# One-hot transfers on a second queue, rounding planned by SyncE's clock, and another key tile in a borrowed buffer

## The chip, the core and the metric

The kernel runs on one core of a Trainium2 chip. The core has TensorE (PE: matrix products and transposes, into PSUM), VectorE (DVE), ScalarE (ACT), GpSimd (POOL) and SyncE (SP), each with its own instruction order, and 16 DMA engines. An instruction waits for semaphores, and all that stands behind it on the same engine waits too. The time is that of one execution on the device in microseconds; the median of a few executions is compared.

## The reference

Attention with routing by clusters, followed by a bilinear feed-forward block. Queries, keys and values are 4 batches x 8 heads x 768 positions x 64.

```
q_assign = argmax(q_n . c_n);  k_assign = argmax(k_n . c_n)     # 16 clusters per head
scores = where(q_assign == k_assign, q k^T / 8, -1e9)
attn = softmax(scores);  x = attn v                             # (B,H,S,D) -> (3072, 512)
out = ((x @ w_a) * (x @ w_b)) @ w_out                           # 512 -> 1536 -> 512
```

A query sees only the keys of its own cluster. The weights w_a, w_b and w_out come as 64-bit numbers and are rounded to 32 bits in the kernel.

## The kernel before

**Pairs of heads.** Two heads are worked on together, which gives 16 pairs. The first six (ND, line 167) are "dense": all 768 x 768 scores are made, the mask is added by a product of one-hot rows, and the exponential is taken. The other ten are "sorted": the rows are scattered by cluster into DRAM (L1509, POOL), loaded again in order (L1539, L1543), small score blocks are made (L1581), weighed (L1606, L1615), written back (L1635) and gathered (L1646).

**A dense pair** has two halves of 384 queries and, for each, six key tiles of 128 (j = 0 to 5). Two key tiles make a group: the scores L592, first by the one-hot rows ohT and then by qkT, into two PSUM tiles; the exponential L605 on ScalarE into a tile pt; the weighing with v, L634; the running sum of the exponentials on VectorE, L623. The tile of the exponential comes from `prob_room` (L579): four buffers of the pool ptp and, for every fifth tile, a stretch of xT that is not in use yet. At the end of a half the denominators are summed (L654) and inverted and applied on VectorE (L674 to L687).

**Pairs 4 and 5** (`by_blocks`) are prepared in 32 x 32 blocks on VectorE: L514 turns queries and keys, L405 makes the similarities, L518 turns these, L522 makes the one-hot rows and L530 turns them. Their 16 rows for each head and quarter then have to go to other partitions, to where the scores read them: eight small DMA transfers for a pair, `move_one_hot` (L492 to L497), all issued by SyncE. The index a is the head of the pair.

**Rounding.** 36 parts of the weights, 128 x 512 each, in the order of `weight_parts` (L1983): eight alternating parts of w_a and w_b for each third of the columns, then w_out's parts 5 to 11 and 0 to 4. For each a DMA into one of two buffers named raw (L300), then on VectorE L311, L314, L318, L321 and L329, and on ScalarE L325 and L326. I call the i-th rounding Ri, counting from 0. A buffer is loaded again when L321 and L325 have read it.

**Feed-forward.** For batch 0 an up product L727 with w_a is copied by ScalarE (L780) and multiplied on VectorE by the product with w_b (L784, which writes h): 24 pairs of products, in two blocks of 384 rows. Then come 21 down products from h and w_out. The first (p1, L1039) adds up over w_out's parts 0 to 5. It carries out all roundings that are left before it is written (`with_weights`, L1770). Later batches use sums of weight blocks kept in DRAM.

**The planner.** The order on each engine is written out by the Python program, with a clock of its own. `now` is the planned time of TensorE. Every engine has a planned clock in `clocks` (V, S, G, P for VectorE, ScalarE, GpSimd and SyncE), which each instruction issued through a `Clocked` object moves on by a fixed cost. Steps of the sorted pairs and roundings are events: `next_round` (L1823) lets rounding i into the order once `arrived[i]` plus a margin has passed and VectorE's clock allows it (`may_round`, L1814), and otherwise asks again 0.5 later. `loaded` (L1795) issues the load of a part and sets `arrived`. So a different planned cost or margin changes which instruction stands behind which, on all engines. SyncE's order holds all plain loads and stores, the reloads of the sorted pairs among them.

Of the kernel before, what the change touches and what calls it, by code (L numbers as in the profile page):

```python
# [34 lines left out]
P = 128  # L35
# [4 lines left out]
def kernel(  # L40
# [91 lines left out]
    with ExitStack() as fast:  # L132
        short_path(nc, tc, fast, c, cn, centroids_in, casts, n_far, q, k, v,
                   moe_w_a, moe_w_b, moe_w_out, out)
# [23 lines left out]
def short_path(nc, tc, ctx, c, cn, centroids_in, casts, n_far, q, k, v,  # L158
# [3 lines left out]
    B, H, S, D = q.shape  # L162
    NC = 16
    DM, DF = moe_w_a.shape
    NJ = S // P
# [5 lines left out]
    HB = S // 2  # L171
# [4 lines left out]
    now, last = [0.0], [0.0]  # L176
    clocks = {"V": 0.0, "S": 0.0, "G": 0.0, "P": 0.0}
    state = (clocks, now, last)
    V, Vs, Vc, Vh, Vm, Vl, Vd = (Clocked(nc.vector, "V", us, *state)
                                 for us in (0.56, 0.19, 0.29, 0.44, 0.7, 0.83, 0.96))  # L180
    S_, Ss, Sl = (Clocked(nc.scalar, "S", us, *state) for us in (0.5, 0.3, 0.85))
    Gi = Clocked(nc.gpsimd, "G", 1.28, *state)
    Q_, Qr, Qc = (Clocked(nc.sync, "P", us, *state) for us in (0.42, 0.62, 2.0))

    def pool(name, bufs, space=None, stack=ctx):
# [108 lines left out]
    raws = {}  # L294

    def load_w(i):
        if i >= len(w_parts):
            return
        raw = rawp.tile([P, WN], INT64, name="raw")
        Q_.dma_start(out=raw, in_=w_parts[i][1])  # L300
        raws[i] = raw
# [79 lines left out]
    qkTs, ohTs, sims = {}, {}, {}  # L381
# [110 lines left out]
    def move_one_hot():  # L492
        while to_move:
            p, ohT, kq, a = to_move.popleft()
            r = 32 * kq + a * NC
            Qr.dma_start(out=ohTs[p][a * D:a * D + NC, kq * HB:(kq + 1) * HB],
                         in_=ohT[r:r + NC, :])  # L497

    def prep_by_blocks(p):

# [28 lines left out]
        def one_hot_across():  # L529
            V.transpose(out=ohT, in_=oh.rearrange("p g c -> p (g c)"))  # L530
            to_move.extend((p, ohT, kq, a) for kq in (0, 2, 3, 1) for a in range(2))
            at(clocks["V"] + 0.6, lambda t: move_one_hot())
# [44 lines left out]
        return p, hf, j  # L577

    def prob_room(u):  # L579
        if u % 5 < 4:  # L580
            return ptp.tile([P, 2, HB], FP32, name="pt")
        return xTs[1][:, HP - 2].rearrange("p (a t) -> p a t", a=2)

    def score(us):
# [17 lines left out]
        def exp():  # L602
            for u, s in zip(us, tiles):
                pt = prob_room(u)
                Sl.activation(out=pt, in_=s[:, :, 0:HB], func=AF.Exp,  # L605
                                     scale=SCALE)
                probs[u] = pt
# [506 lines left out]
    def at(t, f):  # L1114
        heapq.heappush(events, (t, next(serial), f))
# [5 lines left out]
    def begin():  # L1121
        last[0] = now[0]
# [106 lines left out]
    def was(what, n, after=0.0):  # L1229
        return n < 1 or (what, n) in done and done[what, n] + after <= now[0]  # L1230
# [564 lines left out]
    def loaded(i):  # L1795
        while i > done_to[0]:
            done_to[0] += 1
            load_w(done_to[0])
            arrived[done_to[0]] = clocks["V"] if done_to[0] > 21 else now[0]

    done_to = [1]
    arrived = {}

    def round_one(i):
        loaded(i)
        round_w(i)
        if i < 20:
            at(last[0] + 2.5, lambda t: loaded(i + 2))
        else:
            loaded(i + 2)  # L1810
# [3 lines left out]
    def may_round(i):  # L1814
        idle = clocks["V"] <= now[0] + 0.6
        if i < 16:
            return idle or now[0] > 140 + 8.0 * (i - 8) and clocks["V"] <= now[0] + 2.0
        if i < 24:
            return idle or bool(is_late)
        return clocks["V"] <= now[0] + 1.4 and (  # L1820
            was("after", EARLY, 4) if i < 31 else was("put", EARLY - 1, 2))

    def next_round(t):  # L1823
        if not rounds:
            return
        i = rounds[0]
        if not (i in raws and arrived[i] + (4.5 if i < 22 else 3.5) <= now[0] and may_round(i)):
            at(now[0] + 0.5, next_round)
            return
        rounds.pop(0)  # L1830
        begin()
        round_one(i)
        at(max(t + 3.5, now[0]), next_round)

    at(98.0, next_round)
    for n in range(1, NSORT):
        sorted_pair(n, STARTS[n])
# [43 lines left out]
    for g in range(NG + 7):  # L1881
        p, l = divmod(g, GPP)
        if l == 0:
            move_one_hot()
            ready = prep_steps(p + 1)
# [344 lines left out]
```

## Time and profile before

| | us |
|---|---|
| median of 3 runs | 952.77 (952.34 to 955.7) |
| profiled execution | 951.85 |
| its span | 950.1 |
| TensorE busy | 928.4 (98%) |
| VectorE busy | 612.5 (64%) |
| ScalarE busy | 261.5 (28%) |
| POOL busy | 372.8 (39%) |

A row of a timeline reads: start, duration, engine, line and operation, what is written from what, partitions x elements and type, count, and in brackets the idle time of the engine just before with the instruction that ended it. Times count from the start of the span. Rows of a queue (SPq, ACTq) are DMA issues, and their duration is the issuing, not the transfer. A matmul row can hold several matmuls. TensorE's granted clock is 1.00 when it isn't throttled.

### The profile page before, as it was taken

The page shows a single profiled execution, that of the slowest core. Times are in us where ns is not written, and L with a number is a line of the kernel's source. Part 1 is how long each engine was busy: PE and PEld are TensorE (multiplying, and loading weights), DVE is VectorE, ACT ScalarE, POOL GpSimd, SP SyncE. Part 2 cuts the span into 40 slices and gives each one's busy share as a digit, 9 for nine tenths or more (in the row PEclk, how much of TensorE's full clock was granted, in tenths as well). Part 3 has the DMA queues.
Part 4 walks back from the last instruction along what each step waited for, and adds up shares of the span by engine and source line. Part 5 has one row for each costly group of instructions (what it writes and reads, how often), then busy time and mean ns, then how long its engine had stood idle before and what let it go on. Part 6 is the DMA issues. An engine that isn't in the chain of part 4 may idle for free.

```text
span 950.1 us, 20918 instructions
## 1 busy us (share of the span) xinstructions
PE 928.4 (98%) x8068; PEld 492.4 (52%) x8068; DVE 612.5 (64%) x1309; ACT 261.5 (28%) x564; POOL 372.8 (39%) x373
## 2 busy tenths in 40 slices
PE   8999989999999999999999999999999999999997
PEld 5454433434544567554545676545455664444564
DVE  5899988986869886759575945574354433333542
ACT  5876544633433301122212010212221001211100
POOL 1026645665554564555564545555553200000000
PEclk9999999999999999999999999999999999999999
DMA  8967675556799945784688548383825112122311
GB/s 196 243 177 198 175 219 137 161 172 160 185 218 177 206 145 127 158 179 111 147 150 180 165 98 193 96 184 100 165 55 160 37 57 63 56 61 61 113 35 32
DMA packets 293755, 131.82 MB, mean 139 GB/s; under 512 B 230032, under 2 KB 274832, under 8 KB 293648
## 3 DMA queue, kind: packets, MB, share of 16 engines
q1 hardware_dynamic: 281712, 114.23, 49.2%
q0 software_dynamic: 11520, 15.75, 6.1%
q8 instruction: 66, 1.08, 0.5%
q10 hardware_dynamic: 416, 0.43, 0.1%
q14 instruction: 41, 0.34, 0.1%
HBM read 86.93 MB, written 43.20 MB: 137 GB/s over the span
## 4 chain that ended last, share of the span: by engine, by line
PE 80%; DVE 12%; DMA 3%; SPq 2%; issue 2%; ACT 1%; POOL 0%; DVEq 0%; POOLq 0%; ACTq 0%
PE m L727 64%; PE s L592 3%; PE s L1581 3%; PE s L1606 2%; PE O L634 2%; DVE acc L623 2%; PE s L1615 2%; DVE rest L321 1%; PE s L1661 1%; PE m L405 1%; PE O L1367 1%; DVE rest L318 1%; DMA raw<-in_moe_w_out_dram 1%; PE m L654 1%; PE m L1356 1%
## 5 line engine op out<-in xcount | busy, mean ns | idle before, releaser
L1646 POOL DMA_INDIRECT xT<-od,idx x120 | 123.2, 1027 | 110.1 <-PE m L727 80.8
L727 PE MATMUL m<-xT,wa_sb 128*64 128x384 f32 x672 | 116.6, 488 | 2.2 <-DVE h L784 1.4
L727 PE MATMUL m<-xT,wb_sb 128*64 128x384 f32 x672 | 116.5, 488 | 1.3 <-DVE h L784 1.3
L902 DVE TENSOR_TENSOR ha<-ha,m 128x384 f32<-128x384 f32 x72 | 39.7, 551 | 88.0 <-PE m L727 68.4
L899 ACT COPY h<-m 128x384 f32<-128x384 f32 x72 | 34.4, 478 | 194.6 <-PE m L727 194.6
L727 PE MATMUL m<-wo_sb,h 128*64 128x256 f32 x768 | 87.1, 380 | 0.3 <-DVE wo_sb L329 0.3
L902 DVE TENSOR_TENSOR h<-h,m 128x384 f32<-128x384 f32 x72 | 39.7, 551 | 68.7 <-PE m L727 49.3
L1509 POOL DMA_INDIRECT qd<-whole,idx x60 | 58.6, 976 | 59.9 <-PE m L727 41.6
L727 PE MATMUL m<-raw 128*64 128x384 f32 x432 | 79.2, 487 | 1.0 <-DVE raw L864 1.0
L1509 POOL DMA_INDIRECT kvd<-whole,idx x60 | 58.9, 982 | 53.1 <-PE m L727 34.0
L727 PEld LDWEIGHTS m<-xT,wb_sb 128*64 128x64 f32 x672 | 47.4, 137 | 60.4 <-issue 52.0
L727 PEld LDWEIGHTS m<-xT,wa_sb 128*64 128x64 f32 x672 | 47.2, 137 | 60.1 <-issue 52.1
L727 PEld LDWEIGHTS m<-wo_sb,h 128*64 128x64 f32 x768 | 54.4, 137 | 29.0 <-issue 0.8
L727 PE MATMUL m<-xT,h 128*64 128x256 f32 x576 | 64.4, 379 | 0.0
L1509 POOL DMA_INDIRECT qd<-wo_sb,idx x24 | 27.1, 1128 | 74.5 <-DVE acc L623 59.2
L592 PE MATMUL s<-qkT 64*128 64x384 f32 x288 | 53.1, 487 | 0.0
L727 PE MATMUL m<-xT,size 128*64 128x384 f32 x288 | 52.8, 487 | 0.0
L605 ACT ACTIVATE pt<-s 128x768 f32<-128x768 f32 x58 | 44.9, 809 | 28.1 <-PE s L592 26.7
L727 PEld LDWEIGHTS m<-xT,h 128*64 128x64 f32 x576 | 41.3, 137 | 20.7 <-issue 0.2
L1509 POOL DMA_INDIRECT kvd<-h,idx x36 | 40.4, 1123 | 28.3 <-PE s L592 6.9
L727 PEld LDWEIGHTS m<-raw 128*64 128x64 f32 x432 | 30.8, 137 | 38.9 <-issue 35.7
L899 ACT COPY ha<-m 128x384 f32<-128x384 f32 x54 | 25.9, 479 | 87.2 <-PE m L727 86.4
(270 smaller groups left out, 1530.4 us busy)
## 6 DMA issues: line engine op xcount, KB each, us to landing
whole<-kvd SPq DMA_DIRECT2D x80, 160.0 KB
kvd<-xT SPq DMA_DIRECT2D x20, 320.0 KB
whole<-qd SPq DMA_DIRECT2D x40, 160.0 KB
od<-whole SPq DMA_DIRECT2D x40, 160.0 KB
raw<-in_moe_w_a_dram SPq DMA_DIRECT2D x12, 512.0 KB
raw<-in_moe_w_b_dram SPq DMA_DIRECT2D x12, 512.0 KB
raw<-in_moe_w_out_dram SPq DMA_DIRECT2D x12, 512.0 KB
raw<-up_sums SPq DMA_DIRECT2D x96, 64.0 KB
```

What stands on the lines that cost most here:

```text
L592: ins = nc.tensor.matmul(out=s[:, a, 0:HB], lhsT=Ts[p][r, S + j * P:S + (j + 1) * P], rhs=Ts[p][r, hf * HB:(hf + 1) * HB], start=start, st ...
L605: Sl.activation(out=pt, in_=s[:, :, 0:HB], func=AF.Exp, scale=SCALE)
L623: Vd.tensor_tensor(out=acc, in0=probs[u - 1] if j == 1 else acc, in1=probs[u], op=ALU.add)
L634: ins = nc.tensor.matmul(out=O_of[0][a * D:(a + 1) * D, 0:HB], lhsT=vs[p][:, a, j, :], rhs=probs[u][:, a, :], start=(j == 0), stop=(j == N ...
L727: ins = nc.tensor.matmul(out=ps[half], lhsT=lhsT[:, half], rhs=rhs, **kw)
L899: S_.copy(out=box[name], in_=box["X"][:, 0:HB])
L902: V.tensor_tensor(out=box[name], in0=box[name], in1=box[bank][:, 0:HB], op=ALU.add)
L1509: ins = Gi.indirect_dma_start(out=dst[:, :], out_offset=bass.IndirectOffsetOnAxis(ap=M["idx"][:, w, j, a:a + 1], axis=0), in_=src, in_offs ...
L1581: noted(nc.tensor.matmul(out=tiles[s // 2][r0:r0 + m, s % 2, c0:c0 + m], lhsT=M["skT"][r, h, 32 * x:32 * x + m], rhs=M["sqT"][r, h, 32 * x ...
L1606: noted(nc.tensor.matmul(out=ps[:, s, 65 * i:65 * i + 65], lhsT=pt[:, P * i:P * i + P], rhs=vt[:, i, :], start=True, stop=True))
L1615: noted(nc.tensor.matmul(out=ps[r, s, 65 * (2 + i):65 * (3 + i)], lhsT=pt[r, 2 * P + D * i:2 * P + D * i + D], rhs=vt[r, 2 + i, :], start= ...
L1646: paced(Gi.indirect_dma_start(out=M["xs"][:, j, a * D:(a + 1) * D], out_offset=None, in_=od[n][:, :], in_offset=bass.IndirectOffsetOnAxis( ...
```

## The change

Three places. In `move_one_hot` the transfers of head a = 1 are issued by ScalarE through a new object Qs with a planned cost of 0.1, those of head 0 by SyncE as before. In `prob_room` the borrowed stretch of xT holds the key tile j = 2 of every half and no longer every fifth tile. In the planner, the arrival of a part of the weights is no earlier than SyncE's planned clock after the load, and the margin of `next_round` is 7.5 instead of 4.5 for the parts before 12.

```diff
+    Qs = Clocked(nc.scalar, "S", 0.1, *state)
...
-            Qr.dma_start(out=ohTs[p][a * D:a * D + NC, kq * HB:(kq + 1) * HB],
-                         in_=ohT[r:r + NC, :])
+            (Qr, Qs)[a].dma_start(
+                out=ohTs[p][a * D:a * D + NC, kq * HB:(kq + 1) * HB],
+                in_=ohT[r:r + NC, :])
...
     def prob_room(u):
-        if u % 5 < 4:
+        if u % NJ != 2:
             return ptp.tile([P, 2, HB], FP32, name="pt")
...
             load_w(done_to[0])
-            arrived[done_to[0]] = clocks["V"] if done_to[0] > 21 else now[0]
+            arrived[done_to[0]] = max(clocks["P"], clocks["V"] if done_to[0] > 21 else now[0])
...
-        if not (i in raws and arrived[i] + (4.5 if i < 22 else 3.5) <= now[0] and may_round(i)):
+        if not (i in raws and arrived[i] + (7.5 if i < 12 else 4.5 if i < 22 else 3.5) <= now[0] and may_round(i)):
```

## The prediction

> **What bounds the kernel now.** I read the page's busy times first, then TensorE's waits in order of time, and then, around each wait, the timelines of VectorE, ScalarE and SyncE's queue.
>
> ```profile
> span 950.1 us, 20918 instructions
> ...
> PE 928.4 (98%) x8068; PEld 492.4 (52%) x8068; DVE 612.5 (64%) x1309; ACT 261.5 (28%) x564; POOL 372.8 (39%) x373
> ```
>
> TensorE is busy for 928.4 of 950.1 us. What an edit of order can win is therefore at most the 21.7 us in which TensorE stands, and what it can lose is any new place where TensorE stands. The waits of TensorE in the first 300 us that this change can touch are these (timeline of TensorE; the bracket is the idle time and its releaser):
>
> ```profile
> 119.82 0.34 PE L592 MATMUL s<-ohT 64*128 64x384 bf16 x2 [2.38 <-ACT pt L605]
> 120.52 0.34 PE L592 MATMUL s<-ohT 64*128 64x384 bf16 x2 [0.36 <-ACT pt L605]
> ...
> 129.56 1.70 PE L405 MATMUL m<-qkT,cTb 128*32 128x384 f32 x8 [1.16 <-DVE qkT L514]
> 135.84 0.87 PE L654 MATMUL m<-pt,ones 128*64 128x384 f32 x4 [0.68 <-ACT wo_sb L1361]
> 155.94 0.87 PE L654 MATMUL m<-pt,ones 128*64 128x384 f32 x4 [1.54 <-ACT wo_sb L1412]
> 170.93 0.66 PE L1356 MATMUL m<-ident,wo_sb 128*128 128x128 f32 x4 [0.24 <-ACT wo_sb L1361]
> 204.86 2.80 PE L727 MATMUL m<-xT,wb_sb 128*64 128x384 f32 x16 [0.76 <-DVE h L784]
> 210.80 2.80 PE L727 MATMUL m<-xT,wb_sb 128*64 128x384 f32 x16 [0.56 <-DVE h L784]
> ...
> 291.38 2.80 PE L727 MATMUL m<-xT,wa_sb 128*64 128x384 f32 x16 [1.42 <-DVE h L784]
> ```
>
> The first pair, 2.38 + 0.36 = 2.74 us, is the largest. Its cause stands in the queue of SyncE and on VectorE (timelines of SyncE, VectorE, TensorE, then the busy times by stretch, where the column after POOL is the granted clock):
>
> ```profile
> 108.19 5.05 SPq L496 DMA_DIRECT2D ohT<-h  x8
> 113.34 0.53 SPq L300 DMA_DIRECT2D raw<-in_moe_w_a_dram  x1
> ```
> ```profile
> 115.59 0.69 DVE L329 TENSOR_TENSOR wb_sb<-wb_sb,rest 128x512 f32<-128x512 f32 x1
> 117.56 0.43 DVE L311 TENSOR_SCALAR wa_sb<-raw 128x512 int32<-128x512 int32 x1 [1.27 <-DMA raw<-in_moe_w_a_dram]
> ...
> 120.55 0.95 DVE L623 TENSOR_TENSOR acc<-acc,xT 128x768 f32<-128x768 f32 x1
> ```
> ```profile
> 110.58 1.51 PE L634 MATMUL O<-pt,v 128*64 128x384 f32 x8
> ...
> 116.63 0.81 PE L634 MATMUL O<-pt,v 128*64 128x384 f32 x4
> ...
> 120.68 2.06 PE L592 MATMUL s<-qkT 64*128 64x384 f32 x8
> 122.67 2.56 PE L634 MATMUL O<-pt,v 128*64 128x384 f32 x8
> 125.17 0.50 PE L592 MATMUL s<-ohT 64*128 64x384 bf16 x4
> 125.50 1.45 PE L592 MATMUL s<-qkT 64*128 64x384 f32 x8
> ```
> ```profile
> 121.00:125.00 4.00, 4.00 (x16) 1.24 (x12) 3.79 (x10) 1.62 (x2) 0.96 (x1) 0.57 0.99 258
> ```
>
> Eight one-hot transfers take SyncE from 108.19 to 113.24. The raw weights behind them go out at 113.34 and VectorE gets them at 117.56, 4.22 us later. That rounding (call it R8, counting from 0) was put into both VectorE's and ScalarE's order at this point, so the exponentials behind it on ScalarE are late and TensorE stands. Afterwards the granted clock is 0.57 on average in 121 to 125 us: a group of scores takes 2.06 instead of 1.45 us, a weighing 2.56 instead of 1.51, so the pause costs another 0.61 + 1.05 = 1.66 us.
>
> **The change, part by part.** No instruction is added or removed; eight transfers move from SyncE to ScalarE, and the order on every engine moves, since the planner's times feed on each other.
>
> *Key tile in the other room.* The tile with j = 2 of every half uses xT, instead of every fifth. A room of pt is then taken again after 4 instead of 5 tiles for j = 1 and j = 3; for j = 1 the exponential waits for the second addition of the group two back, not the first. One addition is 0.95 us (the row at 120.55); 12 halves give 0 to 11.4 us. I take 0, because in the whole span TensorE waits for an exponential only 3.4 us (row below, from the list of TensorE's waits), 2.74 of it at the place above.
>
> ```profile
> PE s L592 <- ACT pt L605: 3.4, 4, 2.4
> ```
>
> *Transfers by ScalarE.* Four at each of two places. ScalarE's own issue has one near row:
>
> ```profile
> 1.29 0.50 ACTq L259 DMA_DIRECT2D h<-in_k_dram  x1
> ```
>
> So 4 x 0.50 = 2.0 us of ScalarE twice, and SyncE is freed of 4 x 0.63 = 2.5 us twice. At the first place two exponentials stand behind the issues, and TensorE has the weighing, the denominators (L654) and the prefix counts of the sorted pair before it needs their banks; at the second place the transfers also wait for the one-hot transpose (L530), and TensorE has a weighing, one 16-row feed-forward product (2.80) and L654 before the next scores. Hidden, I take 0; if neither cover holds it is 2 x 2.0 us, and no gain is to be had from ScalarE's side.
>
> *Rounding planned later, first effect.* In the changed order R8 stands behind the transposes of pair 5 (L514) and behind L1385 of the sorted pair. The pause at 119.82 goes, with its clock: -2.74 - 1.66. The next wait is then for L514. VectorE ends R7 at 115.59 + 0.69 = 116.28; up to L514 it has what it did from 120.55 to 128.53 (7.98 us) and in addition the end of the index work that stood from 131.81 to 133.69 (1.88):
>
> ```profile
> 131.81 0.57 DVE L1486 TENSOR_TENSOR wo_sb<-wo_sb 128x384 f32<-128x384 f32 x1
> ...
> 133.69 0.57 DVE L311 TENSOR_SCALAR wb_sb<-raw 128x512 int32<-128x512 int32 x1
> ```
> ```profile
> 128.53 1.84 DVE L514 STREAM_TRANSPOSE qkT<-qk 128x768 f32<-128x768 f32 x2
> ```
>
> That starts the first L514 at 126.14 and ends it (1.84 / 2 later) at 127.06. TensorE comes from 116.63 + 0.81 = 117.44, with two groups of scores (0.33 + 1.45), two weighings (1.51) and two sets of transposes L1356 (0.66) ahead of L405: 125.3. It waits 1.7 instead of 1.16: +0.6. The waits of 0.68 and 1.54 go, because L654 no longer stands right behind the bank that ScalarE copies out (the changed order has scores and a weighing, or a product, between): -2.2. Three sets of L1356 now stand with only scores or a weighing between, where the row at 170.93 shows 0.24: 3 x 0.24 = +0.7. The two waits on h (0.76, 0.56) have the same roundings before them in both orders; I let them stand, between gone (-1.3) and doubled (+1.3). The 1.42 at 291.38 came from a raw w_out load behind SyncE's reloads; the changed order has no rounding directly behind such a load there: -1.4. Sum of the first 300 us: -4.4 + 0.6 - 2.2 + 0.7 - 1.4 = -6.7, bounds -10.8 (the pauses above and the clock's 1.66 all gone) and -3 (VectorE's share of them only moved).
>
> *Rounding planned later, second effect.* All 36 roundings must be done before the first down product of batch 0, which adds up over w_out parts 0 to 5; parts 0 to 4 are R31 to R35. Before, R35 alone stands behind the last h (L784). In the changed order R33, R34 and R35 all do, behind two masking steps (L1569) as well, and TensorE's order has only the prefix counts (L1404, L1406) between its last up product and that down product, which carries three separate waits on VectorE. Rows (VectorE, TensorE, SyncE):
>
> ```profile
> 283.99 0.43 DVE L311 TENSOR_SCALAR wo_sb<-raw 128x512 int32<-128x512 int32 x1 [4.71 <-DMA raw<-in_moe_w_out_dram]
> ...
> 297.75 0.82 DVE L1569 TENSOR_TENSOR whole<-whole 128x640 f32<-128x640 f32 x1
> ...
> 325.09 0.56 DVE L784 TENSOR_TENSOR h<-ha,m 128x384 f32<-128x384 f32 x1 [1.87 <-ACT size L325]
> 325.56 0.42 DVE L311 TENSOR_SCALAR wo_sb<-raw 128x512 int32<-128x512 int32 x1
> ...
> 327.20 0.69 DVE L321 SCALAR_TENSOR_TENSOR rest<-raw,rest 128x512 f32<-128x512 uint32 x1
> ...
> 328.54 1.02 DVE L1014 TENSOR_TENSOR ha<-h 128x384 f32<-128x384 f32 x2
> ```
> ```profile
> 281.12 0.36 PE L1404 MATMUL O<-oh_s,before_mine 128*128 128x448 bf16 x1
> ...
> 281.99 2.80 PE L727 MATMUL m<-xT,wb_sb 128*64 128x384 f32 x16
> ...
> 324.91 1.55 PE L1367 MATMUL O<-whole,cTb 128*32 128x192 f32 x16
> 326.39 1.95 PE L727 MATMUL m<-wo_sb,h 128*64 128x256 f32 x16
> 328.67 3.67 PE L727 MATMUL m<-wo_sb,h 128*64 128x256 f32 x32 [0.33 <-DVE wo_sb L329]
> ```
> ```profile
> 278.42 0.62 SPq L300 DMA_DIRECT2D raw<-in_moe_w_out_dram  x1
> ```
>
> Let T be the end of the last up product (324.91 here). h starts 0.18 later and holds VectorE 0.47; two L1569 take 2 x 0.82; a rounding takes 328.54 - 325.56 = 2.98. So R33 runs from T + 2.29 to 5.27, R34 to 8.25. R35's raw load needs the buffer of R33, read for the last time by L321, 327.20 + 0.69 - 325.56 = 2.33 after its start: T + 4.62. A load takes 4.22 (above) or 5.57 (278.42 to 283.99) to arrive. I take 5.57, since that load too stood among SyncE's key and value loads: R35 runs from 10.19 to 13.17, and TensorE goes on 0.13 later, at T + 13.30. Without the wait it would be there at T + 0.87 (281.12 to 281.99) + 1.95 (16 rows from 326.39) = 2.82. So TensorE stands 10.5 us in three pieces, against 0.33 before: +10.15. With 4.22 it is +8.8; with no wait for the load at all (R35 right behind R34) it is +8.2, and this is the floor, as VectorE cannot pass h. Behind it the clock falls as at 121 us: +1.66, bounds 0 and twice that. Nothing covers this: the next work on TensorE without w_out is one product later.
>
> *The rest.* The sorted pairs' chain moves forward: its last transposes (L1661) stand behind 1704 of the 2400 feed-forward matmuls instead of 1716, so POOL's scatters and gathers, which are re-paced with it, set no later end; 0.
>
> *Sum.* 951.85 us is the profiled execution (span 950.1). -6.7 + 10.15 + 1.66 = +5.1 gives 956.95. The median of the runs shown, 952.77, is 0.92 above the profiled one, so I forecast 957.9.
>
> [...] The row says: after pauses of 2.38 and 0.36 us within 3.1 us, mean clock 0.57 over 4 us, price 1.66. [...]
>
> **The rivals.** (a) Not slower: the dense stage gives back everything, 10.8, and the w_out wait stays at its floor without a fall of the clock, 8.2. Place: the first down product against 113 to 292 us. 951.85 - 10.8 + 8.2 + 0.92 = 950.2. It decides from the point where TensorE's waits before the down products shrink by more than its wait there grows. For it: each of those waits has another cause that the new order moves. Against it: VectorE is full there (3.79 of 4 us in 121 to 125), so a wait on it mostly changes place. (b) ScalarE becomes the bound: its issues (4 x 0.50, twice) hold exponentials that TensorE waits for, 957.9 + 4.0 = 961.9. For it: the second set waits for L530. Against: 5 us and more of TensorE's own work behind both places. (c) The half clock lasts twice as long: 957.9 + 1.66 = 959.6. (d) The change does not do what it says: the last roundings are covered after all, so that only the gain is seen, 951.85 - 6.7 + 0.92 = 946.1. Against: the three waits stand in TensorE's order with nothing before them.
>
> **How the numbers follow.** Forecast 0.55 (954 to 961.5), (a) 0.17, (b) 0.11, (c) 0.12, (d) 0.05. A change of under 0.5%, 4.8 us, is about what a measurement of this kernel can't tell from none; the border above is 957.5. A little over half of the forecast's chance, nearly all of (b) and (c): slower 0.50. The rest of it and most of (a): same 0.43. (d) and a tail of (a): faster 0.07. The range goes from (a)'s 950 to beyond (b), 963.
>
> **What would show it.** Right: no wait of TensorE on L605 around 117 us and a clock of 1.00 in 121 to 125; ScalarE's queue with two sets of four L496; three waits of L727 on L329 of wo_sb near 320 us, 9 to 11 us together, with a half clock behind; the rest of the span as before. Wrong: if those three waits come to under 8 us, the floor was misread; if the waits before 300 us do not shrink by 3 us at least, VectorE was the bound of that stage; if ScalarE's L605 are released by the DMA issues and TensorE by L605, it is (b).

## The result and the profile after

| | before | after |
|---|---|---|
| median of 20 runs each | 951.84 us (950.25 to 955.7) | 955.75 us (953.78 to 957.92) |
| ratio of after to before | | 1.0039, 95% interval 1.0032 to 1.0047 |
| profiled execution | 951.85 us | 956.05 us |
| its span | 950.1 us | 954.3 us |

The change costs 3.9 us, 0.4%. The forecast was 957.9 (950 to 963). By the prediction's own border of 957.5 the outcome is the "same" to which it gave 0.43, not the "slower" to which it gave 0.50. The sign is clear of noise all the same: the interval is 0.15% wide, where the prediction took 0.5% to be about what can't be told from nothing. Lines of after stand one or two higher than those of before (L784 is L786, L329 is L330, L592 is L594).

The page of after, its first part, and then the list of TensorE's waits (total, times, longest):

```profile
span 954.3 us, 20910 instructions
...
PE 929.5 (97%) x8068; PEld 493.5 (52%) x8068; DVE 613.3 (64%) x1309; ACT 261.5 (27%) x564; POOL 369.7 (39%) x373
```
```profile
PE m L729 <- DVE wo_sb L330: 8.1, 3, 4.3
PE m L1358 <- DMA wo_sb<-in_q_dram: 2.5, 1, 2.5
PE m L656 <- DVE wo_sb L1387: 1.8, 1, 1.8
PE O L1406 <- DVE oh_s L1393: 1.3, 2, 0.9
...
PE m L1369 <- ACT wo_sb L1363: 0.8, 1, 0.8
...
PE s L594 <- ACT pt L607: 0.7, 2, 0.4
...
PE m L729 <- DVE h L786: 0.2, 1, 0.2
```

TensorE stands 954.3 - 929.5 = 24.8 us instead of 21.7, and is busy 1.1 us longer: together the 4.2 us between the spans. Where it stands is shown by its busy time in stretches, first of before, then of after (from:to, length, busy time of each engine with the number of instructions, TensorE's clock, DMA share and GB/s):

```profile
20.00:100.00 80.00, 79.06 (x565) 37.13 (x557) 72.70 (x135) 57.27 (x110) 25.47 (x23) 1.00 0.73 189
100.00:140.00 40.00, 35.40 (x223) 15.30 (x223) 36.91 (x71) 22.97 (x47) 20.36 (x19) 0.96 0.85 228
140.00:180.00 40.00, 38.22 (x265) 17.02 (x263) 32.45 (x65) 19.93 (x42) 23.25 (x22) 1.00 0.49 140
180.00:260.00 80.00, 78.68 (x620) 36.64 (x619) 65.41 (x127) 32.84 (x71) 46.78 (x45) 1.00 0.63 172
260.00:300.00 40.00, 38.58 (x266) 17.32 (x267) 31.95 (x65) 11.43 (x29) 21.81 (x22) 1.00 1.02 205
300.00:350.00 50.00, 49.67 (x536) 29.41 (x534) 43.25 (x84) 12.86 (x31) 27.78 (x26) 1.00 0.77 188
```
```profile
20.00:100.00 80.00, 78.95 (x565) 37.22 (x561) 72.69 (x135) 58.22 (x111) 24.96 (x23) 1.00 0.74 190
100.00:140.00 40.00, 37.45 (x259) 16.57 (x257) 34.74 (x67) 21.92 (x45) 21.14 (x21) 1.00 0.79 213
140.00:180.00 40.00, 37.40 (x249) 16.45 (x245) 38.32 (x77) 22.17 (x44) 22.25 (x23) 1.00 0.59 177
180.00:260.00 80.00, 79.80 (x649) 38.02 (x647) 65.09 (x124) 31.65 (x74) 46.84 (x46) 1.00 0.65 165
260.00:300.00 40.00, 39.59 (x405) 20.03 (x403) 31.63 (x68) 11.62 (x28) 20.82 (x20) 1.00 0.99 196
300.00:350.00 50.00, 41.07 (x423) 21.83 (x420) 38.49 (x71) 14.24 (x31) 22.75 (x20) 0.90 0.65 163
```

From 20 to 300 us TensorE stands 10.06 us before and 6.81 after: 3.25 us won, and with the clock at 121 us (1.66) 4.9. The clock's part belongs to this execution: in another one of the same kernel (run 5) the pause on the query rows is 3.41 us, and the scores behind it take 2.54 instead of 1.45 us. From 300 to 350 it stands 0.33 before and 8.93 after: 8.6 us lost, behind a clock of 0.90. That is the shape of the forecast. The rows of the two places (timeline of TensorE, then busy time by stretch):

```profile
124.37 0.63 PE L1358 MATMUL m<-ident,wo_sb 128*128 128x128 f32 x4 [2.52 <-DMA wo_sb<-in_q_dram]
...
322.86 0.36 PE L1406 MATMUL O<-oh_s,before_mine 128*128 128x448 bf16 x1 [0.88 <-DVE oh_s L1393]
...
329.14 1.12 PE L729 MATMUL m<-wo_sb,h 128*64 128x256 f32 x4 [4.33 <-DVE wo_sb L330]
332.12 1.12 PE L729 MATMUL m<-wo_sb,h 128*64 128x256 f32 x4 [1.86 <-DVE wo_sb L330]
335.10 5.01 PE L729 MATMUL m<-wo_sb,h 128*64 128x256 f32 x32 [1.86 <-DVE wo_sb L330]
```
```profile
329.14:335.10 5.96, 2.24 (x8) 0.59 (x9) 5.69 (x11) 1.48 (x3) 0.94 (x1) 0.50 0.27 93
335.10:338.00 2.90, 2.90 (x14) 1.69 (x16) 2.90 (x6) 0.65 (x2) 0.00 (x0) 0.53 0.00 0
```

The pause at 119.82 is gone, but a new one stands 4 us behind it, on the query rows. Three pieces of the first down product wait for R33, R34 and R35, the clock is at half in all three (0.50 and 0.53 on average in the two stretches above), and the product behind them takes 5.01 us where before it took 3.67.

### The profile page after: what moved, and what is told of

Read it like the earlier page. It is cut to its first block, busy times and chain, and to the rows that moved or that the text cites. A ratio compares the mean times of both kernels' runs of the same rounds, so it can differ in the third digit from the quotient of the medians.

```text
span 954.3 us, 20910 instructions
## 1 busy us (share of the span) xinstructions
PE 929.5 (97%) x8068; PEld 493.5 (52%) x8068; DVE 613.3 (64%) x1309; ACT 261.5 (27%) x564; POOL 369.7 (39%) x373
## 4 chain that ended last, share of the span: by engine, by line
PE 83%; DVE 10%; DMA 3%; SPq 2%; ACT 1%; issue 1%; DVEq 0%
PE m L729 65%; PE s L594 3%; PE s L1583 3%; PE O L636 3%; PE s L1608 2%; PE s L1617 2%; DVE acc L625 2%; DMA raw<-in_moe_w_out_dram 1%; DVE rest L322 1%; PE s L1663 1%; SPq L1637 1%; PE m L406 1%; PE m L1358 1%; PE m L390 1%; DVE rest L319 1%
## 5 line engine op out<-in xcount | busy, mean ns | idle before, releaser
L729 PE MATMUL m<-wo_sb,h 128*64 128x256 f32 x768 | 89.6, 387 | 8.1 <-DVE wo_sb L330 8.1
L594 PE MATMUL s<-qkT 64*128 64x384 f32 x288 | 52.4, 483 | 0.0
L1511 POOL DMA_INDIRECT kvd<-h,idx x36 | 37.8, 1050 | 28.7 <-PE O L636 8.2
```

Of the source, the lines that this page charges most:

```text
L594: ins = nc.tensor.matmul(out=s[:, a, 0:HB], lhsT=Ts[p][r, S + j * P:S + (j + 1) * P], rhs=Ts[p][r, hf * HB:(hf + 1) * HB], start=start, st ...
L729: ins = nc.tensor.matmul(out=ps[half], lhsT=lhsT[:, half], rhs=rhs, **kw)
L1511: ins = Gi.indirect_dma_start(out=dst[:, :], out_offset=bass.IndirectOffsetOnAxis(ap=M["idx"][:, w, j, a:a + 1], axis=0), in_=src, in_offs ...
```

## The experiments

Every set has runs of the kernel before on its own chip, and ratios go against those: 966.69 us (34 runs) for the first four kernels, 951.62 (23 runs) for the next four, 951.98 (11 runs) for the last two.

**1. Which part makes the stall: the margin undone.** The kernel after with

```diff
-        if not (i in raws and arrived[i] + (7.5 if i < 12 else 4.5 if i < 22 else 3.5) <= now[0] and may_round(i)):
+        if not (i in raws and arrived[i] + (4.5 if i < 22 else 3.5) <= now[0] and may_round(i)):
```

> The kernel after with the margin of next_round back at 4.5 for the parts before 12; transfers by ScalarE, the other key tile and the later arrival stay. The roundings then stand as in the kernel before (R8 ahead of L514 of pair 5, only R35 behind the last h). My theory, that the margin alone makes both the gain before 300 us and the three waits at the first down product: no wait on L329 of wo_sb over 1 us and no half clock there; the pause at 120 us is back, but at most as long as before (2.74 us), since the raw load of R8 now has four and not eight transfers ahead of it on SyncE; 951.8 us to 947.5 us, ratio to before 0.995 to 1.000. Rival, that the transfers by ScalarE, the key tile or the later arrival cost the time: still 954 us and more, ratio over 1.002.

Measured: 962.17 us, ratio 0.9951 (0.9935 to 0.9968). The timeline of TensorE at the two places:

```profile
118.37 0.34 PE L594 MATMUL s<-ohT 64*128 64x384 bf16 x2 [0.36 <-ACT pt L607]
...
122.64 0.63 PE L1358 MATMUL m<-ident,wo_sb 128*128 128x128 f32 x4 [1.20 <-DMA wo_sb<-in_q_dram]
...
331.18 1.08 PE L729 MATMUL m<-wo_sb,h 128*64 128x256 f32 x8 [0.33 <-issue]
```

The stall at the first down product needs the margin: without it no part is waited for. One half of the expectation was wrong. The pause at 120 us did not come back (0.36), since R8 still stands behind L516: it is the later arrival that moves R8, not the margin (run 7 has the arrival alone). So the two effects that the prediction put down to one cause have two.

**2. The stall removed, all else as in after.** From R29 on rounding is let in earlier; up to R28 the order is after's.

```diff
-        return clocks["V"] <= now[0] + 1.4 and (
-            was("after", EARLY, 4) if i < 31 else was("put", EARLY - 1, 2))
+        return clocks["V"] <= now[0] + (1.4 if i < 29 else 4.0) and (
+            was("after", EARLY, 4) if i < 36 else was("put", EARLY - 1, 2))
```

> The kernel after, its order unchanged up to R28; from R29 on a rounding may go into the order when VectorE's planned clock is up to 4.0 ahead (was 1.4), and R31 to R35 no longer wait for the masking of the last sorted pair. R35 then stands ahead of the last h. My theory, that the kernel after has its gain in the dense stage and loses it at the first down product: the waits on L329 of wo_sb fall from 8.05 us to under 1, the clock stays at 1.00 there (1.34 us), the wait of 0.88 us on the prefix counts goes too; the roundings now hold h, which I put at up to 2 us: 955.75 - 10.3 + (0 to 2) = 945.5 to 947.5 us, ratio to before 0.993 to 0.996. Rival, that VectorE is full and the stall only moves to the h waits ahead of the down products: 953 us and more. Rival, that the loss lies in the first 120 us (the 1.1 us by which all is later there): 954 us.

Measured: 962.59 us, ratio 0.995 (0.9932 to 0.9968), against 1.0039 for after, which was measured on another chip. The first down product now has one short wait, and the clock from 318 to 345 us is 1.00:

```profile
327.22 3.67 PE L729 MATMUL m<-wo_sb,h 128*64 128x256 f32 x32 [0.84 <-DVE rest L322]
```

Undoing nothing but the bunch of the last roundings turns a loss of 0.4% into a gain of 0.5%. The rival that the loss lies in the first 120 us falls, and so does the one that it only moves to other waits on VectorE, though a small part does move: behind this product TensorE waits 0.87 and 0.76 us for L1005 and L1016.

**3 and 4. Transfers alone and key tile alone, on top of before.**

```diff
+    Qs = Clocked(nc.scalar, "S", 0.1, *state)
...
-            Qr.dma_start(out=ohTs[p][a * D:a * D + NC, kq * HB:(kq + 1) * HB],
+            (Qr, Qs)[a].dma_start(
```
```diff
-        if u % 5 < 4:
+        if u % NJ != 2:
```

> The kernel before with the transfers of head 1 issued by ScalarE, and nothing else. The order of the roundings is that of the kernel before. My theory: ScalarE's issues are hidden, the raw load of R8 goes out 2.5 us earlier on SyncE, and of the pause at 120 us (2.74 us, with 1.66 us of clock) some 0.3 us is left: 951.84 - 4.1 = 947.7 us; if the exponentials behind ScalarE's issues take its place there: 951.8 us. Rival (ScalarE becomes the bound, four issues of 0.50 us twice): 954 to 956 us, with waits of the scores on the exponentials at both places.

> The kernel before with the key tile j = 2 in the borrowed buffer, and nothing else. My theory: hidden, 951.8 us, ratio 0.999 to 1.001, and the waits of the scores on the exponentials stay at 3.4 us. Rival (a room is taken again after 4 tiles, and the exponential waits for an addition of 0.95 us in each of 12 halves): up to 963 us; 953 us at a tenth of that.

Measured: transfers 967.2 us, ratio 0.9999 (0.9982 to 1.0017); key tile 965.79 us, ratio 0.9997 (0.998 to 1.0013). The key tile does nothing that can be measured, as forecast. The transfers do nothing to the time, but not as I expected. SyncE's queue with the transfers on it (the kernel with the key tile alone), then with four of them moved, and that kernel's waits of SyncE from 100 to 118 us:

```profile
105.64 1.83 SPq L1282 DMA_DIRECT2D kvd<-xT  x2
108.19 5.07 SPq L496 DMA_DIRECT2D ohT<-h  x8
113.36 0.53 SPq L300 DMA_DIRECT2D raw<-in_moe_w_a_dram  x1
```
```profile
109.24 4.45 SPq L1284 DMA_DIRECT2D kvd<-xT  x2
113.79 2.51 SPq L497 DMA_DIRECT2D ohT<-h  x4
116.41 0.53 SPq L301 DMA_DIRECT2D raw<-in_moe_w_a_dram  x1
```
```profile
SPq L1284 <- DMA ohT<-h: 3.4, 1, 3.4
```

SyncE issues four transfers fewer and is later: the store of kvd waits 3.4 us for a transfer that ScalarE issues. The traces have the number of each issue's semaphore. In before, SyncE's issues from 99.19 to 117 us carry eight numbers in turn: 108, 109, 110, 100, 102, 104, 105, 107, then 108 again. In after, ScalarE's four transfers (109.48 to 111.39) carry 108, 109, 110 and 100, and the second store of kvd, issued at 112.91, carries 108 and waits for 108: 3.7 us there for one of ScalarE's transfers, as it is 3.4 in run 3. Of the 3.05 us by which the raw load is later, 1.55 are there before this wait: the loads of the queries (L236) go out at 100.75 and not at 99.20. So the raw load of R8 goes out no earlier than before, and the pause at 120 us is longer here than with the key tile alone:

```profile
123.01 0.50 PE L594 MATMUL s<-ohT 64*128 64x384 bf16 x2 [4.01 <-ACT pt L607]
```
```profile
119.94 0.34 PE L592 MATMUL s<-ohT 64*128 64x384 bf16 x2 [2.43 <-ACT pt L605]
```

**5. The kernel after again**, for a profile beside the next runs.

> The kernel after once more, for a profile beside the runs of this set. My theory: three waits on L329's rows of wo_sb of 8 to 9 us together at the first down product, half clock there, ratio to before 1.003 to 1.005. Rival, that this loss belongs to the other set of runs: ratio under 1.001.

Measured: 956.26 us, ratio 1.0043 (1.003 to 1.0056); the three waits come to 8.0 us again.

**6. TensorE kept busy in the stall**, with transposes into the bank not in use:

```diff
                 for f in range(N2):
+                    for _ in range(warm.pop(0) if warm else 0):
+                        nc.tensor.transpose(out=banks[0][:, 0:P], in_=ident,
+                                            identity=ident)
...
+                warm.extend([0, 0, 24, 10, 10, 0])
                 first()
```

> The kernel after with 24, 10 and 10 transposes (about 0.165 us each, into the bank that is not in use) put into TensorE's order ahead of the three parts that the first down product waits for; their results are not used, and nothing else moves. My theory, that the x32 product at the end of the stall takes 5.01 us only because the clock fell: it takes 3.67 us again, the granted clock stays at 1.00, the three waits shrink to what the transposes leave (about 1 us), and the time falls by 1.3 us against the kernel after, ratio to it 0.998 to 0.999. Rival, that the products behind wait for VectorE anyway (it has the sums of weight blocks to make): no change, 0.9995 to 1.0005.

Measured: 953.83 us, ratio to before 1.0021 (1.0012 to 1.003), 2.4 us less than after in the same set. The last piece and the product behind it, first in the run of after of this set, then with the transposes:

```profile
335.95 6.28 PE L729 MATMUL m<-wo_sb,h 128*64 128x256 f32 x32 [1.86 <-DVE wo_sb L330]
```
```profile
335.33 3.67 PE L731 MATMUL m<-wo_sb,h 128*64 128x256 f32 x32 [1.08 <-DVE wo_sb L330]
```

The pieces end as late as before, for VectorE sets them, but the product behind takes 3.67 us instead of 6.28: 2.61. The clock is 1.00 from 300 to 350 us in run 6, and 0.50 from 330 to 339 us in run 5. So the clock's price is real and here is paid nearly in full: 2.61 us at the product, 2.4 in the median. It was 1.34 in the profiled execution of the result and 2.61 here, so my one number for it (1.66) stood for a spread.

**7. The later arrival alone**, on top of before:

```diff
-            arrived[done_to[0]] = clocks["V"] if done_to[0] > 21 else now[0]
+            arrived[done_to[0]] = max(clocks["P"], clocks["V"] if done_to[0] > 21 else now[0])
```

> The kernel before with the later arrival alone (no earlier than SyncE's planned clock); margin, transfers and key tile as before. R8 then stands behind L514 of pair 5, and only R35 behind the last h. My theory, that moving R8 is the whole gain of the dense stage: no wait of the scores on L605 over 0.5 us at 120 us and no fall of the clock there (2.74 + 1.66 us), no stall at the first down product over 1 us, ratio to before 0.995 to 0.998. Rival, that the pause moves to another wait on VectorE in the same 20 us: ratio 0.999 to 1.001.

Measured: 947.49 us, ratio 0.9953 (0.9941 to 0.9965). The gain of the dense stage is this one line's: from 20 to 300 us TensorE stands 5.95 us, in after 6.81. But the rival was half right as well: the pause at 120 us is gone, and one of 3.54 us stands 8 us behind it, with matmuls at a lower clock (2.35 instead of 1.70 us; 0.91 on average from 100 to 140 us):

```profile
127.84 2.35 PE L405 MATMUL m<-qkT,cTb 128*32 128x384 f32 x8 [3.54 <-DVE qkT L514]
...
328.57 1.08 PE L727 MATMUL m<-wo_sb,h 128*64 128x256 f32 x8 [0.33 <-DVE wo_sb L329]
```

What was won lies in the waits behind (1.54 on L654, 0.76, 0.56 and 1.42 on h), none of which is left in its list.

**8. The kernel after with all transfers on SyncE again** (the diff of run 3 undone, the margin kept).

> The kernel after with all one-hot transfers on SyncE again, and nothing else undone. By the planner's order only R35 then stands behind the last h, though the margin is 7.5. My theory, that the stall comes from the bunch of R33 to R35 and not from a transfer or the margin as such: wait on wo_sb under 3 us at the first down product and a ratio to before of 0.994 to 0.998. Rival, that the margin of 7.5 by itself costs what after lost (or that SyncE with all eight transfers holds the raw loads): 1.002 and more.

Measured: 947.39 us, ratio 0.9965 (0.9944 to 0.9987). Only R35 is behind the last h, and TensorE waits 1.58 us for it. At L405 it waits 3.54 us, as in run 7. Together with run 1: the bunch of R33 to R35 needs both the margin and the transfers by ScalarE; either undone takes it away.

**9 and 10. R7 behind L514.** If VectorE is the bound from 113 to 128 us, then a rounding less in front of L514 takes the wait of run 7 away. Run 9 is run 7 with the first line below; run 10 is run 1 with it, that is with ScalarE's transfers and the other key tile.

```diff
-    due = {g: [i] for i, g in enumerate((1, 3, 4, 6, 11, 17, 20, 22))}
+    due = {g: [i] for i, g in enumerate((1, 3, 4, 6, 11, 17, 20, 25))}
```

> The kernel before with the later arrival alone (as in the run with the arrival alone) and R7 due at group 25 instead of 22, so that it stands behind L514 and L518 of pair 5 on VectorE; transfers, margin and key tile as before. My theory, that VectorE is the bound between 113 and 128 us: L514 starts a rounding (2.98 us) earlier and L405 waits at most 0.8 us for it instead of 3.54, its matmuls are back at 1.70 us (were 2.35 at a lower clock); the product with w_b, which needs R7, comes five groups of matmuls later and does not wait; the tail is unchanged. 3 to 3.5 us less than the run with the arrival alone: ratio to before 0.990 to 0.993. Rival, that the wait is passed on to the next thing that VectorE makes (the first product with w_b, the scores, or h): ratio 0.995 to 0.997.

> The same R7 at group 25, in the kernel after with the margin back at 4.5: arrival, transfers by ScalarE and the other key tile stay. It differs from the run before it in the transfers and the key tile. My theory, that ScalarE's transfers hold SyncE's second store of kvd (the waits name it for 3.4 to 3.7 us) and so delay the query rows: a wait of L1358 on a DMA of the query rows of 1 to 3.5 us near 123 us, which the run before it does not have, and a time 1 to 3 us above that run's. Rival, that the transfers are hidden: the same time within 0.5 us and no such wait.

Measured: run 9 944.92 us, ratio 0.994 (0.9921 to 0.996); run 10 946.66 us, ratio 0.9939 (0.9922 to 0.9955). Run 9, and below it run 10:

```profile
124.20 1.70 PE L405 MATMUL m<-qkT,cTb 128*32 128x384 f32 x8 [0.46 <-DVE qkT L514]
```
```profile
123.71 0.63 PE L1358 MATMUL m<-ident,wo_sb 128*128 128x128 f32 x4 [2.52 <-DMA wo_sb<-in_q_dram]
...
124.61 2.61 PE L594 MATMUL s<-qkT 64*128 64x384 f32 x8
```

In run 9 the wait of 3.54 falls to 0.46 and the matmuls are back at 1.70 us, with VectorE as busy from 113 to 128 us (14.24 us, in run 7 14.25), so VectorE was the bound there. The ratio is just outside what I expected (0.990 to 0.993), and its interval overlaps that of run 7; that it is faster than run 7 isn't settled by the times. A part of what was won comes back as a wait of 1.5 us on L654, which run 7 doesn't have. In run 10 the wait on the query rows is there, which run 9 doesn't have, but the times (1.7 us apart, intervals on top of each other) don't tell the two. That the transfers cost time by this wait is shown as a wait, not as a time. Run 9 has the lowest median, 7 us below the kernel before (5.7 by the ratio), with only the arrival and the due time of R7 changed.

## Why the prediction was right, and where its steps were off

- **The gain before 300 us: -6.7 forecast, -4.9 found** (3.25 of waits and 1.66 of clock). It is within the bounds, and the waits shrank by just more than the 3 us below which VectorE was to be the bound of that stage. The pause at 120 us and its clock went, as did 0.68, 1.54 and 1.42; the waits on h, which I left standing, fell from 0.76 + 0.56 to 0.20. What failed are the steps "+0.6 for L405" and "3 x 0.24" for the sets of transposes. I had TensorE spend two of these sets ahead of L405. They do stand there in after, but the first of them waits itself, 2.52 us, for the query rows, and L405 (L406 there) behind them waits for nothing. Where no set stands ahead (runs 7 and 8), the wait for L514 is 3.54 us, not 1.7. The 0.24 was read from a place where the rows had long been there. Two waits that I had not named came in too: 0.8 on L1363 and 1.8 on L1387.
- **Transfers by ScalarE: "hidden, 0", and SyncE "freed of 2.5 us twice".** ScalarE's side was right: in all of after the scores wait 0.7 us for exponentials (list above; both waits stand at 36 us). SyncE's side was wrong: its waits in after from 100 to 118 us show it held for 3.7 us by the transfers that it no longer issues. I costed the queue that they leave by their number and not by what the semaphore that they share with it (108 in after) ties together. In time it is nothing by itself (run 3, ratio 0.9999), but the query rows are late with it: TensorE waits 2.52 us for them in after and in run 10, and not at all in run 9.

```profile
SPq L1284 <- DMA ohT<-h: 3.7, 1, 3.7
```

- **Key tile: 0.** Right (run 4).
- **The second effect, the stall: +10.15 forecast; 8.05 + 0.88 us standing, less 0.33, found, and 1.2 us more in the two x4 pieces at half clock (2 x 1.12 instead of 2 x 0.54): +9.8.** The mechanism was right; that the size was right too is in part luck, since two errors cancel. The load of R35 was not waited for: it went out at 328.43 and its data were there by 331.59, 3.16 us later, where I took 5.57 and, as the lower case, 4.22. So R33, R34 and R35 follow each other without a gap, which is the case of the floor, 1.94 us less than I took. And VectorE began R33 at 326.02, 4.04 us behind the last up product and not 2.29, because h itself came late, behind steps of the sorted pair (L1554, L1393): 1.75 us more. The three waits come to 8.05 us, just over the floor of 8 and under the 9 to 11 that I had named as the sign. The cause was named too broadly: it is not the rounding planned by SyncE's clock that bunches the last three, but the margin together with the move of the transfers to another planned clock (runs 1, 7 and 8). No run tells ScalarE's planned cost of 0.1 from SyncE's planned clock, which the move makes earlier. The end of the last up product on TensorE, h, R33 and R35 on VectorE, the load of R35 on SyncE's queue, and ScalarE's first step of R35:

```profile
319.23 2.75 PE L729 MATMUL m<-xT,wb_sb 128*64 128x384 f32 x16
```
```profile
324.08 0.55 DVE L786 TENSOR_TENSOR h<-ha,m 128x384 f32<-128x384 f32 x1
...
326.02 0.42 DVE L312 TENSOR_SCALAR wo_sb<-raw 128x512 int32<-128x512 int32 x1
...
331.99 0.42 DVE L312 TENSOR_SCALAR wo_sb<-raw 128x512 int32<-128x512 int32 x1
```
```profile
328.43 0.33 SPq L301 DMA_DIRECT2D raw<-in_moe_w_out_dram  x1
```
```profile
331.59 0.67 ACT L326 ACTIVATE size<-raw 128x512 f32<-128x512 f32 x1 [7.53 <-DMA raw<-in_moe_w_out_dram]
```

- **The clock: 1.66 forecast, 1.34 in the profiled execution, 2.61 in the next.** The clock was at half for 10.24 us in the one, until 337.85, and for 13.65 us in the other, until 341.27. Rival (c), the half clock for twice as long, adds a second 1.66 us that no run shows; in its place the runs showed whole prices of 1.34 and 2.61 us, on both sides of the forecast's 1.66 and under the rival's 3.32.
- **The sum.** +5.1 forecast, 4.2 between the profiled executions, 3.9 between the medians. -4.9 + 9.8 + 1.34 = +6.2; two waits behind 350 us (0.98 on L864, 0.7 on L1037) are gone, -1.7, which I had as "the rest of the span as before". Of the remaining -0.3 I can't say more. Another 0.9 of the forecast's 2.1 us above the result is the median I started from, 952.77 of three runs, where twenty give 951.84.
- **Rival (d)**, the gain without the stall, 946.1: not what the change does, but runs 2, 7 and 8 show what it would have been, 0.4 to 0.5% below before.

## What to carry to other kernels

When a planner writes the order, a move of four transfers to a planned clock that counts 0.1 for each, and 3 us more of margin, both meant for work at 120 us, can bunch other work 200 us later: cost a change of such numbers by the written order of the whole program, and look above all at what stands between the last input and the first instruction that needs everything. Four transfers moved to ScalarE's queue were not free for SyncE's, which they left: it waited 3.4 us for one of them in run 3 and 3.7 in after, so see which semaphores two queues share. Where an engine is full for 15 us (here VectorE, busy for 14.25 of them in run 7), look for the wait behind the one that you take away: here it moved by 8 us (run 7), and taking work away from in front of it (R7) shrank it to 0.46 us (run 9).

## What the runs showed of the hardware that I had not expected

**The same pause, with and without a fall of the clock.** In after TensorE stood 2.52 us at 121.85 and the scores behind ran at 1.00; in run 10 it stood 2.52 us in the same place, and the clock behind was 0.63 over 4 us, with 2.61 us for a group of 1.45. The clock records of the traces show where the two differ. In each profiled execution the clock changes only at steps of 3.41 us: it stays at half for 3.41 us in before and in run 10, 6.83 in run 7, 10.24 in after and 13.65 in run 5 (at the first down product). At full clock the records of before run for 116.05 and 822.61 us, those of after for 317.44 and 614.40: 34, 241, 93 and 180 such steps. Cut at these steps, the pause of after lies in two, with 0.96 us of standing in the first and 1.56 in the second; the pause of run 10 lies almost whole in one, with 2.36 us, and the next step is at half clock. Busy time by step, of after and of run 10:

```profile
119.39:122.81 3.42, 2.45 (x16) 0.75 (x12) 3.15 (x14) 1.99 (x3) 1.92 (x2) 1.00 1.05 293
122.81:126.22 3.41, 1.85 (x14) 1.27 (x16) 3.20 (x8) 0.68 (x2) 0.96 (x1) 1.00 1.15 282
```
```profile
121.35:124.76 3.41, 1.05 (x10) 0.85 (x12) 3.22 (x9) 0.75 (x2) 0.25 (x1) 1.00 1.05 250
124.76:128.17 3.41, 3.41 (x14) 1.43 (x10) 2.35 (x3) 1.82 (x3) 1.66 (x2) 0.50 1.05 298
```

Over all twelve profiled executions, without the first 10 and the last 20 us of each, the clock fell 14 times. In 13 of these TensorE had stood for 1.96 to 3.30 us of the step before (2.17 in before, 2.80 in after); in one (run 8, the wait for R35) for 1.58. The most that a step at full clock held without a fall behind it was 1.83 us (after, at 171 us). So the length of a pause alone does not tell the outcome, and what decides between 1.58 and 1.83 us is open.

In run 1 a fall came after 2.07 us of standing, on the product behind a wait for h (4.31 us instead of 2.80, with a clock of 0.66 from 201 to 206 us):

```profile
201.05 4.31 PE L729 MATMUL m<-xT,wb_sb 128*64 128x384 f32 x16 [2.07 <-DVE h L786]
```

**One chip was 1.6% slower with the same kernel.** The kernel before took 966.69 us on the chip of the first set and 951.6 to 952.0 on the others. In the kernel with the key tile alone, whose order is nearly that of before, the span is 13.5 us longer (963.6), 5.4 of it by the wait on L864 (at 399.17 instead of 393.76) and 8.1 behind it; TensorE has gaps there that the profile puts down to nothing that it shows ("issue", 1.65 us in five places at L1581 from 600 us on). Why is open; ratios to the kernel before of the same chip are not touched by it.
